# Compact weight and right-hand-side tails in a chain of attention and two gated feed-forward layers

## The chip, the cores and the metric

The kernel runs on one core of a Trainium2 chip. The metric is the device time of one execution in microseconds; the median of several runs counts. TensorE (PE) multiplies matrices, VectorE (DVE) and ScalarE (ACT) work on elements, SyncE (SP) issues nearly all transfers from one queue, in order.

## The reference

```python
x = mlstm(q, k, v, i_gate, f_gate, o_gate)       # (4, 8, 768, 40) -> 3072 tokens x 320
g = sigmoid(x @ moe_w_gate) * (x @ moe_w_val)    # 320 -> 1536
x = g @ moe_w_out                                # 1536 -> 320
h = x @ moe2_w_in                                # 320 -> 2048
y = (h * clip(h + 3, 0, 6) / 6) @ moe2_w_out     # 2048 -> 320
```

`mlstm` is an attention-like recurrence over 768 steps with decays, for 32 heads; it is computed in six chunks of 128 steps.

## The kernel before

Every matmul takes its operands as a high and a low part (`hi` is a cast, `lo` the value minus the cast), and three products of parts are added. An inner size of 320 is two full blocks of 128 rows and a tail of 64; the tail's high and low parts are stacked into one operand of 128 rows.

First come the chunks 0 to 5. In chunk c the steps (c, f), f from 0 to 11, do the first layer: `m1_h` (lines 552 to 559), the gate (line 578, 579), `split_g`, and one or two steps later `m1_out` (lines 594, 604). `m1_end(c)` copies the three output banks into the tile `x2` with line 610 and lines 613 to 615 and stores it in `x2_dram`; it is emitted in step 1 of the next chunk. Between the steps stand pieces of the next chunk's attention (`att0`, `att1`, `att2`: scores, the decays' scan at line 386, their weighing at line 401, transposes at line 534).

Beside this the weights are converted. `work`, one job every second step in the chunks 2 to 4, fetches a pair of 64-bit words, turns it into float32 (`to_f32`, lines 99 to 119) and stores it in `w2_dram` (`store_w2`, line 619): first the eight blocks of `moe2_w_in`, then the eight of `moe2_w_out`. The input layer of the second feed-forward is done in seven products instead of eight for each pair of chunks (a Strassen form of two by two blocks). So each weight block needs four sums (S1 to S4) of its four parts. `combine_w2`, in every second step from chunk 3 on, loads a block back, its tail four times over by transfers of 32 rows (lines 651, 656), forms the sums (line 663), splits them (lines 667, 668, 673) and stores two pieces in `ws_dram` (line 677). The tiles of these pieces, `x2`, and later `w2f` and `o`, have the tag `x2` with two buffers in common.

Then come three pairs of chunks. For each pair seven right-hand sides (`B11`, `B21`, `T1`, `T2`, `B22`, `T3`, `T4`) are formed from `x2_dram`: `x_load` loads four main parts, `x_combine` forms sums (line 843) and splits them (lines 838, 839), and in a second call does the same for the tails, which it loads four times over by transfers of 32 rows (lines 815, 833, 834). For pair 0 this stands in chunk 5, for the others at the end of the pair before. A pair runs eight groups: `load_group` brings the seven weights of a group (line 686), `product` (line 920) multiplies, `gate2` gates, `m2_out` (lines 957 to 959) is the output layer. The gated values of the pair's second chunk are kept and run through `m2_out` at the pair's end, one group after another; there the right-hand sides of the next pair are made.

The order on the engines is a planner's, which takes the program's order as priority and its own estimates of time; `tc.issue_after(gate)` keeps a job behind the gate of its step. A tile with a tag waits for the release of the buffer that it takes.

Of the kernel before, what the change touches and what calls it, by code (L numbers as in the profile page):

```python
# [24 lines left out]
P = 128  # L25
# [7 lines left out]
def mlstm_then_two_gated_ffn(  # L33
# [51 lines left out]
    w2_dram = dram.tile([F2, P, 640], F32, name="w2_dram")  # L85
    ws_dram = dram.tile([F2 // 2, P, 7, 3 * P], F32, name="ws_dram")
# [17 lines left out]
    def to_f32(r, u=None):  # L104

        lower = r.bitcast(I32).rearrange("p (n two) -> p two n", two=2)[:, 0, :]
        u = scaled(r) if u is None else u
        bits = cpool.tile([P, 640], I32, tag="bits", name="bits")
        nc.vector.tensor_scalar(
            out=bits, in0=u.bitcast(I32), scalar1=3, scalar2=None, op0=ALU.logical_shift_left
        )
        nc.vector.scalar_tensor_tensor(
            out=bits, in0=lower, scalar=29, in1=bits,  # L120
            op0=ALU.logical_shift_right, op1=ALU.bitwise_or,
        )
        return bits.bitcast(F32)
# [35 lines left out]
    def hi_out1(key, x):  # L159

        w = new_slot(key)
        nc.scalar.copy(out=w[:, :, 0:320], in_=x.rearrange("p (j n) -> p j n", j=2))
        return w

    def lo_out1(w, x):
        wf = w.bitcast(F32)
        r = x.rearrange("p (j n) -> p j n", j=2)
        nc.vector.tensor_tensor(
            out=w[:, :, 320:384], in0=r[:, :, 256:320], in1=wf[:, :, 256:320], op=ALU.subtract
        )  # L170
        nc.vector.tensor_tensor(
            out=w[:, :, 384:640], in0=r[:, :, 0:256], in1=wf[:, :, 0:256], op=ALU.subtract
        )
# [444 lines left out]
    def store_w2(n, x):  # L618
        nc.sync.dma_start(out=w2_dram[n], in_=x)
# [7 lines left out]
    for n in [*range(0, F2, 2), *range(1, F2, 2)]:  # L627
        jobs.append(((wo2 if n % 2 else w2)[n // 2], store_w2, n))
# [9 lines left out]
    def load_out2(n):  # L638
        x = xpool.tile([P, 640], F32, tag="x2", name="w2f")
        nc.sync.dma_start(out=x, in_=w2_dram[2 * n + 1])  # L640
        split_out2(("out2", n), x)

    A11, A12, A21, A22, S1, S2, S4 = range(7)
    S3 = A21

    def combine_w2(n):


        src = w2_dram[2 * n]
        a = cpool.tile([P, 7, 2, P], F32, tag="wa", name="wa", bufs=1)  # L650
        nc.sync.dma_start(
            out=a[:, 0:4, 0, :], in_=src[:, 0:512].rearrange("p (ik c) -> p ik c", c=P)
        )
        tail = src[:, 512:640].rearrange("(ik r) c -> r ik c", r=32)
        for r in range(0, P, 32):
            nc.sync.dma_start(out=a[r : r + 32, 0:4, 1, :], in_=tail)
        for to, x, y, op in (
            (S1, A21, A22, ALU.add),
            (S2, S1, A11, ALU.subtract),
            (S3, A11, A21, ALU.subtract),  # L660
            (S4, A12, S2, ALU.subtract),
        ):
            nc.vector.tensor_tensor(out=a[:, to], in0=a[:, x], in1=a[:, y], op=op)
        for k, m in ((0, 4), (4, 3)):
            st = xpool.tile([P, 4, 3, P], F32R, tag="x2", name="ws")
            sf = st.bitcast(F32)
            nc.scalar.copy(out=st[:, :m, 0:3:2, :], in_=a[:, k : k + m])
            nc.vector.tensor_tensor(
                out=st[:, :m, 1, :], in0=a[:, k : k + m, 0, :], in1=sf[:, :m, 0, :], op=ALU.subtract
            )  # L670
            for r in (32, 96):
                q = slice(r, r + 32)
                nc.vector.tensor_tensor(
                    out=st[q, :m, 2, :], in0=a[q, k : k + m, 1, :], in1=sf[q, :m, 2, :],
                    op=ALU.subtract,
                )
            nc.sync.dma_start(
                out=ws_dram[n, :, k : k + m, :],
                in_=sf[:, :m].rearrange("p s t c -> p s (t c)"),
            )  # L680
# [3 lines left out]
    def load_group(n):  # L684
        t = xpool.tile([P, 7, 3, P], F32R, tag="x", name="wg")
        nc.sync.dma_start(
            out=t.bitcast(F32).rearrange("p s t c -> p s (t c)"), in_=ws_dram[n]
        )
        w_groups.append(t)
# [101 lines left out]
    combined = 0  # L791

    def x_load(pair):


        def rows():
            return late.tile([P, T], F32, tag="c", name="xr", bufs=11)

        main, tail = {}, {}
        for k in range(2):  # L800
            for j in range(2):
                src = x2_dram[2 * pair + j]
                main[k, j], tail[k, j] = rows(), None
                nc.sync.dma_start(out=main[k, j], in_=src[:, k, :])
        return pair, main

    def x_combine(loads, tail):
        pair, b = loads
        if tail:
            b = {}  # L810
            for k in range(2):
                for j in range(2):
                    b[k, j] = late.tile([P, T], F32, tag="c", name="xr", bufs=11)
                    for r in range(0, P, 32):
                        nc.sync.dma_start(
                            out=b[k, j][r : r + 32],
                            in_=x2_dram[2 * pair + j, 32 * k : 32 * k + 32, 2, :],
                        )
        else:
            xsets.append(  # L820
                {
                    key: late.tile([P, 3, T], F32R, tag="X", name="X", bufs=7)
                    for key in ("B11", "B21", "T1", "T2", "B22", "T3", "T4")
                }
            )
        xs = xsets[-1]
        b11, b12, b21, b22 = b[0, 0], b[0, 1], b[1, 0], b[1, 1]

        def put(key, v):
            x = xs[key]  # L830
            xf = x.bitcast(F32)
            if tail:
                nc.scalar.copy(out=x[:, 2, :], in_=v)
                nc.vector.tensor_tensor(
                    out=x[64:, 2, :], in0=v[64:], in1=xf[64:, 2, :], op=ALU.subtract
                )
            else:
                nc.scalar.copy(out=x[:, 0, :], in_=v)
                nc.vector.tensor_tensor(out=x[:, 1, :], in0=v, in1=xf[:, 0, :], op=ALU.subtract)

        def minus(x, y, out=None):
            out = late.tile([P, T], F32, tag="c", name="xr", bufs=11) if out is None else out
            nc.vector.tensor_tensor(out=out, in0=x, in1=y, op=ALU.subtract)
            return out

        put("B11", b11)
        put("B21", b21)
        t1 = minus(b12, b11)
        put("T1", t1)
        t2 = minus(b22, t1)  # L850
        put("T2", t2)
        put("B22", b22)
        put("T3", minus(b22, b12, b12))
        put("T4", minus(b21, t2))

# [10 lines left out]
    for i, (c, f, ts) in enumerate(steps):  # L866
# [20 lines left out]
        if c == 0:  # L887
            work(1 if i < 2 * halves[0] else 2, n_w1)
        elif c < NC - 1:

            with tc.issue_after(gate):
                work(c > 1 and f % 2 == 0, n_jobs)
                if c > 2 and f % 2 and combined < F2 // 2:
                    combine_w2(combined)
                    combined += 1
        elif f == 0:
            assert not jobs and not pieces and combined == F2 // 2
            early_sb.close()
            late = ctx.enter_context(tc.tile_pool(name="late", bufs=1, reuse_waits="tile"))
            x_loads = x_load(0)  # L900
            load_group(0)
        else:
            if f > 1 and f - 2 < F2 // 2:
                load_out2(f - 2)
            if f in (2, 5):
                x_combine(x_loads, f > 2)
# [10 lines left out]
    def product(ps, w, s, x, first):  # L917

        for i, (a, b) in enumerate(((2, 2), (0, 1), (1, 0), (0, 0))):
            nc.tensor.matmul(  # L920
                out=ps, lhsT=w[:, s, a, :], rhs=x[:, b, :], start=first and i == 0, stop=i == 3,
                skip_group_check=True,
            )

    def sbuf_copy(ps):
        t = late.tile([P, T], F32, tag="c", name="c", bufs=11)
        nc.scalar.copy(out=t, in_=ps)
        return t
# [47 lines left out]
    for pair in range(NC // 2):  # L976
# [4 lines left out]
        for n in range(NG):  # L981
# [30 lines left out]
            if n == NG - 2 and pair + 1 < NC // 2:  # L1012
                x_loads = x_load(pair + 1)
# [6 lines left out]
        for n in range(NG):  # L1020
            for j in range(2):
                m2_out(cb, n, j, split_g(kept[n][:, j]))
            if more and n in (0, 2):
                x_combine(x_loads, n > 0)
# [6 lines left out]
def _layout(q, k, v, i_gate, f_gate, o_gate, moe_w_gate, moe_w_val, moe_w_out, moe2_w_in, moe2_w_out):  # L1031
# [17 lines left out]

    def pairs(w):  # L1050
# [5 lines left out]
    w2 = moe2_w_in.reshape(DM, F2 // 2, 2, P)  # L1056
# [6 lines left out]
        "w2": words(rows_in(w2[:, :, 0].reshape(DM, -1), w2[:, :, 1].reshape(DM, -1))),  # L1063
# [23 lines left out]
```

## Time and profile before

| | |
|---|---|
| median of 3 runs | 861.96 us (860.65 to 863.66) |
| profiled execution, its own time | 860.47 us |
| its span, first to last instruction | 858.6 us |
| PE, DVE, ACT busy share | 97%, 70%, 48% |
| mean granted clock | 0.997 |

The span is what the trace covers. Busy shares are means over stages that differ: chunk 2 runs from about 226 us, chunk 3 from about 306, chunk 4 from about 396, chunk 5 to about 524, the pairs from there on. Matmuls are pipelined, so that a single one is shown longer (0.39 us for 512 columns) than the distance to the next one.

### The profile page before, as it was taken

To read this page: it belongs to the slowest core of one execution; us is meant where nothing else is said; L and a number is where in the kernel's file an instruction comes from. 1 tells how busy PE (TensorE), PEld (TensorE's weight loads), DVE (VectorE), ACT (ScalarE), POOL (GpSimd) and SP (SyncE) were. 2 spreads that over 40 slices of the span, in tenths; PEclk is the share of its full clock that TensorE was granted. 3 is DMA by queue.
4 is the path that set the end of the run, shared out by engine and by line. 5 is a ranking of instruction groups with operands and counts; after the bars stand their busy time and mean duration, and the time that the engine had idled before them with its cause. 6 is when DMAs were issued, how large, how long until landed. Compare 5 with 4: busy or idle time off the path is not lost.

```text
span 858.6 us, 17204 instructions
## 1 busy us (share of the span) xinstructions
PE 829.1 (97%) x7109; PEld 710.1 (83%) x7109; DVE 603.7 (70%) x1086; ACT 413.2 (48%) x821; POOL 2.5 (0%) x8
## 2 busy tenths in 40 slices
PE   6599899999999999998999999999999999999998
PEld 6489689888788787786888888888998889988898
DVE  7899975775576678988956734656766668665653
ACT  3687733322333343444425524656546555555542
POOL 1000000000000000000000000000000000000000
PEclk9999999999999999999999999999999999999999
DMA  9635733322555368887623503434404454033300
GB/s 345 234 126 198 260 98 111 126 94 73 173 171 165 124 241 265 274 268 254 208 99 116 156 1 110 177 138 177 144 32 142 159 199 144 32 129 134 124 31 32
DMA packets 41534, 130.65 MB, mean 152 GB/s; under 512 B 4592, under 2 KB 16048, under 8 KB 38384
## 3 DMA queue, kind: packets, MB, share of 16 engines
q1 hardware_dynamic: 41408, 129.45, 43.9%
q8 instruction: 56, 0.92, 0.4%
q14 instruction: 22, 0.18, 0.1%
q10 hardware_dynamic: 48, 0.10, 0.0%
HBM read 104.53 MB, written 25.00 MB: 151 GB/s over the span
## 4 chain that ended last, share of the span: by engine, by line
PE 79%; DVE 13%; DMA 4%; issue 2%; ACT 1%; SPq 0%; DVEq 0%; ACTq 0%
PE acc L594 9%; PE mm L920 9%; PE mm L558 6%; PE mm L556 6%; PE mm L557 6%; PE att L920 4%; PE acc L920 4%; PE mm L552 4%; PE acc L604 3%; PE mm L559 3%; PE mm L959 2%; PE mm L957 2%; PE acc L957 2%; PE mm L958 2%; PE acc L959 2%
## 5 line engine op out<-in xcount | busy, mean ns | idle before, releaser
L565 ACT CAST gh<-g 128x512 fp32r<-128x512 f32 (+1 forms) x130 | 76.4, 588 | 132.2 <-DVE g L579 110.4
L556 PE MATMUL mm<-x,w 128*128 128x512 f32 (+1 forms) x328 | 121.0, 369 | 0.0
L557 PE MATMUL mm<-x,w 128*128 128x512 f32 (+1 forms) x328 | 120.8, 368 | 0.0
L558 PE MATMUL mm<-x,w 128*128 128x512 f32 (+1 forms) x328 | 120.4, 367 | 0.0
L566 DVE TENSOR_TENSOR gl<-g,gh 128x512 fp32r<-128x512 f32 (+1 forms) x130 | 84.1, 647 | 51.2 <-ACT gh L565 50.8
L594 PE MATMUL acc<-gh,w 128*128 128x512 f32 (+1 forms) x328 | 104.4, 364 | 0.1
L920 PE MATMUL mm<-X,wg 128*128 128x512 f32 x336 | 84.3, 391 | 0.0
L579 DVE TENSOR_TENSOR g<-g,mm 128x512 f32<-128x512 f32 (+1 forms) x82 | 50.4, 615 | 34.6 <-PE mm L559 34.2
L920 PEld LDWEIGHTS mm<-X,wg 128*128 128x128 f32 x336 | 61.9, 188 | 12.6 <-DVE g L936 0.3
L557 PEld LDWEIGHTS mm<-x,w 128*128 128x128 f32 x328 | 62.8, 191 | 10.7
L558 PEld LDWEIGHTS mm<-x,w 128*128 128x128 f32 x328 | 62.6, 191 | 10.6
L556 PEld LDWEIGHTS mm<-x,w 128*128 128x128 f32 x328 | 62.8, 191 | 8.4
L594 PEld LDWEIGHTS acc<-gh,w 128*128 128x128 f32 x328 | 60.6, 189 | 10.7 <-ACT x L610 0.9
L552 PE MATMUL mm<-x,w 128*128 128x512 f32 (+1 forms) x164 | 66.8, 408 | 2.5 <-DVE cst L523 1.6
L578 ACT ACTIVATE g<-mm 128x512 f32<-128x512 f32 (+1 forms) x82 | 44.5, 543 | 44.0 <-PE mm L559 41.8
L386 DVE TENSOR_TENSOR_SCAN dec<-dec,ident 128x512 f32<-128x512 f32 x40 | 48.0, 1215 | 21.3 <-DMA dec<-fz_dram 21.3
L559 PE MATMUL mm<-x,w 128*128 128x512 f32 (+1 forms) x164 | 59.9, 365 | 0.0
L594 PE MATMUL acc<-gl,w 128*128 128x512 f32 (+1 forms) x164 | 59.8, 365 | 0.0
L935 ACT ACTIVATE gb<-c,half 128x512 f32<-128x512 f32 x48 | 34.6, 724 | 44.0 <-DVE c L931 43.7
L566 DVE TENSOR_TENSOR gl<-gb,gh 128x512 fp32r<-128x512 f32 x48 | 32.4, 690 | 24.2 <-ACT gh L565 24.1
L565 ACT CAST gh<-gb 128x512 fp32r<-128x512 f32 x48 | 29.5, 620 | 36.5 <-PE att L958 35.1
L920 PE MATMUL att<-X,wg 128*128 128x512 f32 x168 | 46.3, 395 | 0.0
(188 smaller groups left out, 1737.9 us busy)
## 6 DMA issues: line engine op xcount, KB each, us to landing
wg<-ws_dram SPq DMA_DIRECT2D x24, 1344.0 KB, 5.7
raw<-in_w SPq DMA_DIRECT2D x20, 640.0 KB, 4.3
qk<-in_qkT SPq DMA_DIRECT2D x22, 512.0 KB, 5.0
vko<-in_vko SPq DMA_DIRECT2D x22, 480.0 KB, 4.4
dec<-fz_dram SPq DMA_DIRECT2D x20, 512.0 KB, 5.8
raw<-in_wo SPq DMA_DIRECT2D x14, 640.0 KB, 4.5
ws_dram<-ws SPq DMA_DIRECT2D x8, 768.0 KB, 3.6
w_dram<-bits SPq DMA_DIRECT2D x16, 320.0 KB, 2.4
```

Source lines behind the costliest of these rows:

```text
L386: nc.vector.tensor_tensor_scan(out=x, data0=a["factors"][n] if "factors" in a else x, data1=ident4.rearrange("p h l -> p (h l)"), initial= ...
L552: nc.tensor.matmul(out=banks[j], lhsT=tail, rhs=xl[:, 2, :], start=True, stop=False)
L556: nc.tensor.matmul(out=banks[j], lhsT=hi, rhs=xh[:, k, :], start=False, stop=False)
L557: nc.tensor.matmul(out=banks[j], lhsT=hi, rhs=xl[:, k, :], start=False, stop=False)
L558: nc.tensor.matmul(out=banks[j], lhsT=lo, rhs=xh[:, k, :], start=False, stop=False)
L559: nc.tensor.matmul(out=banks[j], lhsT=tail, rhs=xh[:, 2, :], start=False, stop=True)
L565: nc.scalar.copy(out=gh, in_=g)
L566: nc.vector.tensor_tensor(out=gl, in0=g, in1=gh.bitcast(F32), op=ALU.subtract)
L578: gate = nc.scalar.activation(out=g, in_=banks[0], func=AF.Sigmoid).ins
L579: nc.vector.tensor_tensor(out=g, in0=g, in1=banks[1], op=ALU.mult)
L594: nc.tensor.matmul(out=a[m], lhsT=lhsT, rhs=rhs, start=st and lhsT is hi and rhs is gh, stop=en and lhsT is lo, skip_group_check=True,)
L920: nc.tensor.matmul(out=ps, lhsT=w[:, s, a, :], rhs=x[:, b, :], start=first and i == 0, stop=i == 3, skip_group_check=True,)
```

## The change

The layout of `moe2_w_in` on the host puts the tail of each block as 4 x 32 rows of 32 columns beside its four main parts, so that the four parts lie in one tile [128, 7 x 160] after conversion, with room for the three sums. `combine_w2` is now the job's own second half: it takes the converted tile, with no way through DRAM, and forms four sums of 160 columns. It writes all high parts to one tile and all low parts to another, and stores of each the main part in `ws_dram` and the tail in rows 0 to 31 or 32 to 63 of `wt_dram`. `load_group` reads the main parts with one transfer and the stack of 64 rows twice.

The jobs alternate between a block of `moe2_w_in` and one of `moe2_w_out`; the extra calls in the chunks 3 and 4 are gone. For the right-hand sides `x_load` loads the tails packed as [128, 128] beside the main parts, sums are formed over 640 columns, and `put` splits the packed tail, stores it in `xt_dram` and reads it back with four transfers into the 128 rows of its operand. `x_combine` is a generator that makes one right-hand side at each call, one per step of chunk 5 and one per group at a pair's end. The tag `c` has 7 buffers of 640 columns instead of 11 of 512.

```diff
+    wt_dram = dram.tile([F2 // 2, 64, 7, P], F32, name="wt_dram")
+    xt_dram = dram.tile([NC // 2, 7, 2, 4, 32, P], F32, name="xt_dram")
+    ws_dram = dram.tile([F2 // 2, P, 2, 7 * P], F32, name="ws_dram")
...
-        bits = cpool.tile([P, 640], I32, tag="bits", name="bits")
+        tile_ = cpool.tile([P, 7 * 160], I32, tag="bits", name="bits")
+        bits = tile_[:, 0:640]
...
+    def combine_w2(n, x):
+        a = x.rearrange("p (s c) -> p s c", s=7)
         for to, x, y, op in (
             (S1, A21, A22, ALU.add),
             (S2, S1, A11, ALU.subtract),
...
             (S4, A12, S2, ALU.subtract),
         ):
             nc.vector.tensor_tensor(out=a[:, to], in0=a[:, x], in1=a[:, y], op=op)
+        hi, lo = [xpool.tile([P, 7 * 160], F32R, tag="x2", name="ws") for _ in range(2)]
+        main, tail = [
+            (a[:, :, k:m], [t[:, 7 * k : 7 * m].rearrange("p (s c) -> p s c", s=7) for t in (hi, lo)])
+            for k, m in ((0, P), (P, 160))
+        ]
+        for v, (h, _) in (main, tail):
+            nc.scalar.copy(out=h, in_=v)
+        for v, (h, l) in (main, tail):
+            nc.vector.tensor_tensor(out=l, in0=v, in1=h.bitcast(F32), op=ALU.subtract)
+        for k, t in enumerate((hi, lo)):
+            tf = t.bitcast(F32)
+            nc.sync.dma_start(out=ws_dram[n, :, k], in_=tf[:, : 7 * P])
+            nc.sync.dma_start(
+                out=wt_dram[n, 32 * k : 32 * k + 32].rearrange("r s (q c) -> q r s c", q=4),
+                in_=tf[:, 7 * P :].rearrange("p (s c) -> p s c", s=7),
             )
...
+    for n in range(F2 // 2):
+        jobs.append((w2[n], combine_w2, n))
+        jobs.append((wo2[n], store_w2, n))
...
+        t = xpool.tile([P, 3, 7, P], F32R, tag="x", name="wg")
+        tf = t.bitcast(F32).rearrange("p a s c -> p a (s c)")
+        nc.sync.dma_start(out=tf[:, 0:2], in_=ws_dram[n])
+        for r in (0, 64):
             nc.sync.dma_start(
+                out=tf[r : r + 64, 2], in_=wt_dram[n].rearrange("r s c -> r (s c)")
             )
...
+                t = b[k, j] = late.tile([P, 640], F32, tag="c", name="xr", bufs=7)
+                nc.sync.dma_start(out=t[:, 0:T], in_=src[:, k, :])
+                for q in range(4):
+                    nc.sync.dma_start(
+                        out=t[32 * q : 32 * q + 32, T:],
+                        in_=src[32 * k : 32 * k + 32, 2, q * P : (q + 1) * P],
+                    )
+        return x_combine(pair, b)
...
+        def put(key, v):
+            x = xs[key] = late.tile([P, 3, T], F32R, tag="X", name="X", bufs=7)
+            t = late.tile([P, 2, P], F32R, tag="xt", name="xt", bufs=3)
+            xf, tf = x.bitcast(F32), t.bitcast(F32)
+            nc.scalar.copy(out=t[:, 0, :], in_=v[:, T:])
+            nc.vector.tensor_tensor(out=t[:, 1, :], in0=v[:, T:], in1=tf[:, 0, :], op=ALU.subtract)
+            d = xt_dram[pair, len(xs) - 1]
+            nc.sync.dma_start(out=d.rearrange("k q r t -> (q r) k t"), in_=tf)
+            for k in range(4):
+                nc.sync.dma_start(
+                    out=xf[32 * k : 32 * k + 32, 2, :].rearrange("r (q t) -> r q t", q=4),
+                    in_=d[k // 2].rearrange("q r t -> r q t"),
+                )
+            nc.scalar.copy(out=x[:, 0, :], in_=v[:, 0:T])
+            nc.vector.tensor_tensor(
+                out=x[:, 1, :], in0=v[:, 0:T], in1=xf[:, 0, :], op=ALU.subtract
             )
...
-                if c > 2 and f % 2 and combined < F2 // 2:
-                    combine_w2(combined)
-                    combined += 1
...
-            if f in (2, 5):
-                x_combine(x_loads, f > 2)
+            next(x_parts, None)
...
-            if more and n in (0, 2):
-                x_combine(x_loads, n > 0)
+            if more:
+                next(x_parts, None)
```

## Rows read from the trace of the kernel before

**Rows 1.** The page, busy time of the engines over the span.

```profile
PE 829.1 (97%) x7109; PEld 710.1 (83%) x7109; DVE 603.7 (70%) x1086; ACT 413.2 (48%) x821; POOL 2.5 (0%) x8
```

**Rows 2.** Busy time by stretch: length, PE, PEld, DVE, ACT, POOL, granted clock, DMA share, GB/s.

```profile
226.00:306.00 80.00, 80.00 (x878) 64.01 (x877) 55.52 (x105) 28.30 (x58) 0.00 (x0) 1.00 0.50 164
306.00:330.00 24.00, 24.00 (x248) 19.12 (x248) 19.63 (x37) 12.63 (x23) 0.00 (x0) 1.00 0.69 236
330.00:372.00 42.00, 40.93 (x432) 32.73 (x432) 39.74 (x76) 17.38 (x34) 0.00 (x0) 1.00 0.79 262
372.00:402.00 30.00, 27.62 (x225) 20.86 (x223) 28.45 (x51) 12.98 (x23) 0.00 (x0) 0.94 0.80 272
```

**Rows 3.** Waits of TensorE from 300 to 402 us: total, times, longest.

```profile
PE att L534 <- DVE dec L401: 3.2, 2, 2.2
```

**Rows 4.** TensorE in order of time: start, length, instruction, idle time before it.

```profile
396.04 0.55 PE L534 MATMUL att<-ident,yo 128*128 128x128 f32 x3 [2.23 <-DVE dec L401]
...
398.42 0.63 PE L557 MATMUL mm<-x,w 128*128 128x512 f32 x1
399.19 0.80 PE L594 MATMUL acc<-gh,w 128*128 128x512 f32 x1
```

**Rows 5.** Busy time by stretch, behind the stall (columns as in rows 2).

```profile
396.00:400.00 4.00, 3.83 (x11) 2.62 (x12) 4.00 (x6) 2.36 (x6) 0.00 (x0) 0.57 0.82 284
```

**Rows 6.** The chain that ended last, around 395 us: start, length, what.

```profile
393.00 5.53 DMA ws_dram<-ws
...
398.55 0.59 ACT x L610
```

**Rows 7.** Busy time by stretch, end of the first pair (columns as in rows 2).

```profile
600.00:636.00 36.00, 35.18 (x233) 34.23 (x232) 26.93 (x44) 19.26 (x35) 0.00 (x0) 1.00 0.27 87
```

**Rows 8.** Busy time on tiles `wa` (twice) and `xr`: DVE, ACT, clock, DMA share, GB/s.

```profile
200.00:460.00 260.00, 41.85 (x80) 14.38 (x16) 0.99 0.58 195
...
306.00:402.00 96.00, 29.88 (x56) 10.81 (x12) 0.98 0.77 259
...
430.00:745.00 315.00, 43.62 (x66) 24.81 (x42) 1.00 0.35 122
```

**Rows 9.** Groups of VectorE by shape: busy us, mean ns, idle before.

```profile
L179 DVE TENSOR_TENSOR w<-w2f,w 128x640 fp32r<-128x640 f32 x8 | 6.6, 823 | 5.1 <-ACT w L178 5.1
...
L168 DVE TENSOR_TENSOR w<-bits,w 128x128 fp32r<-128x128 f32 x6 | 1.7, 278 | 0.0
```

**Rows 10.** Waits from 160 to 163 us.

```profile
PE att L534 <- DVE dec L401: 1.6, 1, 1.6
```

**Rows 11.** Transfers by line: count, KB each, median us from issue to landing.

```profile
w_dram<-bits SPq DMA_DIRECT2D x16, 320.0 KB, 2.4
...
xr<-x_dram SPq DMA_DIRECT2D x48, 64.0 KB, 2.1
...
wa<-w_dram SPq DMA_DIRECT2D x8, 256.0 KB, 5.5
wa<-w_dram SPq DMA_DIRECT2D x32, 64.0 KB, 4.2
```

**Rows 12.** ScalarE in order of time, change from chunk 2 to chunk 3.

```profile
296.70 0.60 ACT L578 ACTIVATE g<-mm 128x512 f32<-128x512 f32 x1 [2.25 <-PE mm L559]
...
306.48 0.59 ACT L610 COPY x<-acc 128x512 f32<-128x512 f32 x1 [1.58 <-PE acc L594]
...
308.69 0.58 ACT L614 COPY sw<-acc 64x512 f32<-64x512 f32 x1
```

**Rows 13.** TensorE in order of time, first output product of chunk 3.

```profile
312.40 0.39 PE L594 MATMUL acc<-gh,w 128*128 128x512 f32 x1
```

**Rows 14.** Line 815, issues on SP's queue: ns min/median/max.

```profile
L815 SPq DMA_DIRECT2D xr<-x_dram x48: 302/419/1837, 456.7 to 726.3; - x48
```

**Rows 15.** SP's queue in order of time, last groups of the first pair.

```profile
583.97 1.95 SPq L804 DMA_DIRECT2D xr<-x_dram  x4
593.81 10.23 SPq L686 DMA_DIRECT2D wg<-ws_dram  x2
```

More of the change, by code (lines that the diff above doesn't have):

```diff
@@ L84, in mlstm_then_two_gated_ffn @@
     x2_dram = dram.tile([NC, P, 3, T], F32, name="x2_dram")
-    w2_dram = dram.tile([F2, P, 640], F32, name="w2_dram")
-    ws_dram = dram.tile([F2 // 2, P, 7, 3 * P], F32, name="ws_dram")
+    wo2_dram = dram.tile([F2 // 2, P, 640], F32, name="wo2_dram")
+    wt_dram = dram.tile([F2 // 2, 64, 7, P], F32, name="wt_dram")
+    xt_dram = dram.tile([NC // 2, 7, 2, 4, 32, P], F32, name="xt_dram")
+    ws_dram = dram.tile([F2 // 2, P, 2, 7 * P], F32, name="ws_dram")
     slots = {}
@@ L122, in to_f32 @@
         )
-        return bits.bitcast(F32)
+        return tile_.bitcast(F32)
     def new_slot(key):
@@ L161, in hi_out1 @@
         w = new_slot(key)
-        nc.scalar.copy(out=w[:, :, 0:320], in_=x.rearrange("p (j n) -> p j n", j=2))
+        nc.scalar.copy(out=w[:, :, 0:320], in_=x[:, 0:640].rearrange("p (j n) -> p j n", j=2))
         return w
@@ L166, in lo_out1 @@
         wf = w.bitcast(F32)
-        r = x.rearrange("p (j n) -> p j n", j=2)
+        r = x[:, 0:640].rearrange("p (j n) -> p j n", j=2)
         nc.vector.tensor_tensor(
@@ L618, in store_w2 @@
     def store_w2(n, x):
-        nc.sync.dma_start(out=w2_dram[n], in_=x)
+        nc.sync.dma_start(out=wo2_dram[n], in_=x[:, 0:640])
+    A11, A12, A21, A22, S1, S2, S4 = range(7)
+    S3 = A21
+    def combine_w2(n, x):
+        a = x.rearrange("p (s c) -> p s c", s=7)
+        for to, x, y, op in (
+            (S1, A21, A22, ALU.add),
+            (S2, S1, A11, ALU.subtract),
+            (S3, A11, A21, ALU.subtract),
+            (S4, A12, S2, ALU.subtract),
+        ):
+            nc.vector.tensor_tensor(out=a[:, to], in0=a[:, x], in1=a[:, y], op=op)
+        hi, lo = [xpool.tile([P, 7 * 160], F32R, tag="x2", name="ws") for _ in range(2)]
[14 more added lines that the diff above has]
+            )
     jobs = []
@@ L626, in mlstm_then_two_gated_ffn @@
     n_w1 = len(jobs)
-    for n in [*range(0, F2, 2), *range(1, F2, 2)]:
-        jobs.append(((wo2 if n % 2 else w2)[n // 2], store_w2, n))
+    for n in range(F2 // 2):
+        jobs.append((w2[n], combine_w2, n))
+        jobs.append((wo2[n], store_w2, n))
     jobs.reverse()
@@ L639, in load_out2 @@
         x = xpool.tile([P, 640], F32, tag="x2", name="w2f")
-        nc.sync.dma_start(out=x, in_=w2_dram[2 * n + 1])
+        nc.sync.dma_start(out=x, in_=wo2_dram[n])
         split_out2(("out2", n), x)
[L643 to L680, printed above, removed]
     w_groups = []
     def load_group(n):
[L685 to L688, printed above, removed]
+        t = xpool.tile([P, 3, 7, P], F32R, tag="x", name="wg")
[5 more added lines that the diff above has]
+            )
         w_groups.append(t)
@@ L790, in mlstm_then_two_gated_ffn @@
     xsets = []
-    combined = 0
     def x_load(pair):
-        def rows():
-            return late.tile([P, T], F32, tag="c", name="xr", bufs=11)
-        main, tail = {}, {}
+        b = {}
         for k in range(2):
@@ L802, in x_load @@
                 src = x2_dram[2 * pair + j]
[L803 to L824, printed above, removed]
-            )
[L826 to L839, printed above, removed]
@@ new lines, in x_load, with x_combine @@
+                t = b[k, j] = late.tile([P, 640], F32, tag="c", name="xr", bufs=7)
[4 more added lines that the diff above has]
+                        in_=src[32 * k : 32 * k + 32, 2, q * P : (q + 1) * P],
+                    )
+        return x_combine(pair, b)
+    def x_combine(pair, b):
+        b11, b12, b21, b22 = b[0, 0], b[0, 1], b[1, 0], b[1, 1]
+        xs = {}
+        xsets.append(xs)
+        def put(key, v):
[7 more added lines that the diff above has]
+            for k in range(4):
+                nc.sync.dma_start(
+                    out=xf[32 * k : 32 * k + 32, 2, :].rearrange("r (q t) -> r q t", q=4),
+                    in_=d[k // 2].rearrange("q r t -> r q t"),
+                )
+            nc.scalar.copy(out=x[:, 0, :], in_=v[:, 0:T])
+            nc.vector.tensor_tensor(
+                out=x[:, 1, :], in0=v[:, 0:T], in1=xf[:, 0, :], op=ALU.subtract
+            )
@@ L841, in minus @@
         def minus(x, y, out=None):
-            out = late.tile([P, T], F32, tag="c", name="xr", bufs=11) if out is None else out
+            out = late.tile([P, 640], F32, tag="c", name="xr", bufs=7) if out is None else out
             nc.vector.tensor_tensor(out=out, in0=x, in1=y, op=ALU.subtract)
@@ L846, in x_combine @@
         put("B11", b11)
+        yield
         put("B21", b21)
+        yield
         t1 = minus(b12, b11)
         put("T1", t1)
+        yield
         t2 = minus(b22, t1)
         put("T2", t2)
+        yield
         put("B22", b22)
+        yield
         put("T3", minus(b22, b12, b12))
-        put("T4", minus(b21, t2))
+        yield
+        put("T4", minus(b21, t2, b21))
+        yield
     n_two = n_first + len(tile_steps(1))
@@ L892, in mlstm_then_two_gated_ffn @@
                 work(c > 1 and f % 2 == 0, n_jobs)
-                if c > 2 and f % 2 and combined < F2 // 2:
-                    combine_w2(combined)
-                    combined += 1
         elif f == 0:
-            assert not jobs and not pieces and combined == F2 // 2
+            assert not jobs and not pieces
             early_sb.close()
             late = ctx.enter_context(tc.tile_pool(name="late", bufs=1, reuse_waits="tile"))
-            x_loads = x_load(0)
+            x_parts = x_load(0)
             load_group(0)
@@ L920, in product @@
             nc.tensor.matmul(
-                out=ps, lhsT=w[:, s, a, :], rhs=x[:, b, :], start=first and i == 0, stop=i == 3,
+                out=ps, lhsT=w[:, a, s, :], rhs=x[:, b, :], start=first and i == 0, stop=i == 3,
                 skip_group_check=True,
@@ L925, in sbuf_copy @@
     def sbuf_copy(ps):
-        t = late.tile([P, T], F32, tag="c", name="c", bufs=11)
+        t = late.tile([P, 640], F32, tag="c", name="c", bufs=7)[:, 0:T]
         nc.scalar.copy(out=t, in_=ps)
@@ L1012, in mlstm_then_two_gated_ffn @@
             if n == NG - 2 and pair + 1 < NC // 2:
-                x_loads = x_load(pair + 1)
+                x_parts = x_load(pair + 1)
         more = pair + 1 < NC // 2
@@ L1048, in rows_in, with rows_combined @@
         return np.concatenate([main, tail], axis=2)
+    def rows_combined(w):
+        w = w.reshape(DM, -1, 2, P)
+        main = w[: 2 * P].reshape(2, P, -1, 2, P).transpose(2, 1, 3, 0, 4)
+        tail = w[2 * P :].reshape(2, 32, -1, 2, 4, 32).transpose(2, 4, 1, 3, 0, 5)
+        n = main.shape[0]
+        parts = [main.reshape(n, P, 4, P), tail.reshape(n, P, 4, 32)]
+        return np.concatenate(parts, axis=3).reshape(n, P, 640)
     def pairs(w):
@@ L1054, in words @@
         return np.ascontiguousarray(w).view(np.int64)
-    w2 = moe2_w_in.reshape(DM, F2 // 2, 2, P)
     return {
@@ L1062, in _layout @@
         "wo1": words(pairs(moe_w_out)),
-        "w2": words(rows_in(w2[:, :, 0].reshape(DM, -1), w2[:, :, 1].reshape(DM, -1))),
+        "w2": words(rows_combined(moe2_w_in)),
         "wo2": words(pairs(moe2_w_out)),
```

## The prediction

> **What bounds the kernel now.** The engine table of the page comes first: TensorE is busy 829.1 of 858.6 us [rows 1]. The change touches no matmul: the same products, with the same shapes, read the same values from another place. It can therefore only give back time in which TensorE waits, or add some. The second view is the busy time by stage [rows 2]. From 226 to 330 us TensorE has no idle time at all; from 330 to 402 it loses 1.07 and 2.38 us. In the two stretches that lose, VectorE (DVE) is busy 39.74 of 42 and 28.45 of 30 us, 95% of both; in the two that don't, it is at 69 and 82%. That is the reading on which this prediction rests: over the whole span VectorE is no bound, but it is the bound for these 72 us, and that is where the combinations of the weights stand (line 663 and lines 667 to 673).
>
> The third view says what those waits were. TensorE waited twice for line 401, the weighing of the scores on VectorE, 3.2 us in all [rows 3]; the longer wait is 2.23 us, ahead of the transposes at 396.04 [rows 4]. Behind the stall the clock falls: from 396 to 400 us the granted clock is 0.57 of full, a mixture of the two levels of 1.2 and 2.4 GHz, so 4.0 x 0.43 = 1.7 us more are lost [rows 5]. The chain of waits shows a second cause at the same place: the store of a combined weight, issued at 393.00, takes 5.53 us, and ScalarE's copy at line 610 starts only when it has landed [rows 6], because the copied tile has the store's tile as its buffer; line 594 on TensorE starts behind that copy, at 399.19, 0.77 us after the matmul before it [rows 4]; I put 0.3 us of that down to the copy, the rest to the slow clock. The sum that this stage loses: 3.2 + 1.7 + 0.3 = 5.2 us. More than that the change can hardly win. What else TensorE waits for lies in the first 161 us, where it adds nothing, or at the end of the pairs (36.00 - 35.18 = 0.8 us each [rows 7]), where a gate's own chain ends.
>
> **The weights' half.** Eight combinations cost VectorE 41.85 us and ScalarE 14.38 [rows 8], so 5.23 and 1.80 each. An operation's price over its columns comes from two rows with 128 and 640 columns, 0.278 and 0.823 us [rows 9]: 0.142 us + 1.064 ns a column. After: four sums of 160 columns at 0.312 = 1.25 us, one subtraction of 896 at 1.095, one of 224 at 0.38: 2.73 us, 2.5 less per combination. ScalarE casts 1120 columns instead of 1792: 1.1 instead of 1.8 us. Where they stand matters more. Before, six fall into one chunk (306 to 402 us); after, each stands behind its conversion in the same job, three in chunk 2, three in chunk 3, two in chunk 4. In the 96 us from 306 to 402, VectorE's 19.63 + 39.74 + 28.45 = 87.8 us hold 29.88 us of the combinations' work [rows 2, 8]; with four in their place (the first of chunk 4 starts within them) it is 87.8 - 29.9 + 10.9 = 68.8, or 72%. Chunk 2 (226 to 306 us) goes from 55.5 to 55.5 + 8.2 = 63.7 of 80, 80%. Both lie below the 82% at which TensorE didn't wait. So VectorE's backlog goes, and the lateness of line 401 with it.
>
> Not all of that wait need go. At 160 us TensorE waits 1.6 us for the same line 401 where no combination stands [rows 10]. On SP's queue a job now has four stores in place of one store, five loads and two stores; they wait for ScalarE and VectorE as those did, with the attention's loads queued behind them, for whose decays line 401 waits in turn. Four issues fewer and 40 loads of 4 MB less [rows 11] speak for earlier loads, not later ones. I keep 0.5 us of the 5.2 as left over.
>
> **The tails' stores.** Two of the four stores go in runs of 32 values: 4 x 32 x 7 = 896 runs of 128 bytes. The trace has no such run. The nearest rows: 64 KB in 32 runs land in 2.1 us, 64 KB in 128 runs in 4.2, 256 KB in 512 runs in 5.5 [rows 11]. From the first to the second a run costs (4.2 - 2.1) / 96 = 22 ns, from the second to the third 1.3 / 384 = 3.4 ns; that gives 2.1 + 896 x 0.022 = 21.8 us at most and 2.1 + 896 x 0.0034 = 5.1 us at least. I take 5.1, by the row whose number of runs is nearest to 896. What waits for it: `hi`, `lo` and the next chunk's `x2` share two buffers, and the combination of each chunk's step 0 stands one step ahead of line 610's copies into `x2`. On ScalarE the next step's sigmoid is queued behind those copies, and TensorE waits for both. Chunk 3 gives the times: its step 0 converts behind the gate at 296.70 [rows 12]; I estimate 6 us for conversion, combination, casts and the issue of both stores of `hi`, so 302.9. Line 610 starts at 306.48, the last copy of that block ends at 308.69 + 0.58 = 309.27 [rows 12], and TensorE takes the bank again at 312.40 [rows 13]. So the copies may start 3.1 us late, at 309.6: a store that lands within 309.6 - 302.9 = 6.7 us costs nothing. With 5.1 us it is covered, by 1.6 us. If that cover goes, each of three chunk changes pays the excess.
>
> **The right-hand sides' half.** VectorE spent 43.62 us and ScalarE 24.81 on them [rows 8]. After: 12 differences of 640 columns (0.823), 21 subtractions of 512 (0.687) and 21 of 128 (0.278): 9.9 + 14.4 + 5.8 = 30.1 us, 13.5 less. At a pair's end VectorE is busy 26.93 of 36 us while TensorE loses 0.8 [rows 7], so this is worth nothing. SP's queue pays for it: each tail is now stored and read back by four transfers. Seven tails a pair are 7 x 5 issues of 0.42 us [rows 14] and seven waits for a store, 2.4 us each as the store of converted weights [rows 11]: 7 x (2.1 + 2.4) = 31.5 us. While SP waits, the next tail, a group's load or an output's store is queued behind it. The stage has 36 us, and the work can start before it: the sixteen tail loads now go with the four main loads, 20 x 0.42 = 8.4 us from 583.97 in a queue that had nothing else to issue until 593.81 [rows 15]. The seventh tail is read by the seventh product of the next pair, not at its start; pair 0 has chunk 5, twice as long. Cost 0, with the last tail's way as the other bound: 2.4 + 4 x 0.42 + 2.1 = 6.2 us a pair. Seven buffers of 640 columns in place of eleven hold four loads and one group's three copies, just enough, and `load_group` issues three transfers a whole group ahead: 0 both.
>
> **The sum.** 5.2 - 0.5 = 4.7 us less, from 860.47 to 855.8 us for the profiled execution, whose own time is 1.49 us under the median of the runs. Against the median: 861.96 - 4.7 = 857.3 us. A measurement of this kernel tells about 0.3%, 2.6 us, from no change.
>
> **Rivals.** First, the wait comes back elsewhere: line 401 is late because its decays are, as at 160 us [rows 10], or the copies of line 610 wait at more chunk changes than before. Against it: VectorE had hardly a pause in the stretches that lost. Some 2 us of gain stay: 860 us.
>
> Second, slower: the tails' stores land late. If the 896 runs of a store pass through a quarter of the DMA engines, the 3.0 us that they take above the first 2.1 become 12, and a store lands in 14.1 us. Line 610 is then 14.1 - 6.7 = 7.4 us too late at three chunk changes: 22.2 - 4.7 = 17.5 us slower, 879 us. It outweighs the gain from a landing of 6.7 + 4.7 / 3 = 8.3 us. For it: line 610 waits for such a store already [rows 6], and the upper bound is 21.8 us. Against: the planner may put the copies ahead of the combination, and 22 ns a run comes from loads that went beside others. The Trainium skill speaks for it ("DMA: Bandwidth & Descriptors", the section on why a DMA increments its semaphore by 16 and not by 1): a transfer runs on the largest number of engines up to 16 that divides the slowest dimension of both sides, here 4 on the DRAM side, so on 4 of 16. By that rule the time is this rival's 879 us; no run here shows a transfer whose slowest dimension is under 16.
>
> Third, the right-hand sides' round trip is too long, and the last tails come late at two pair starts. At half the bound, 3 us each, it is 857.3 + 6 = 863.3 us.
>
> **Chances and range.** Forecast (4.7 us, give or take 2) 0.53; first rival 0.21; third 0.08; second 0.18. Faster by over 0.3% is the forecast, 0.53; within 0.3% the first and third, 0.29; slower the second, 0.18. The range runs from the whole 5.2 us and the median's scatter of 1.3 us below it, 855.4, to a landing of 9.6 us, 3 x (9.6 - 8.3) = 4 us above the time before, 866. Alone, the forecast's own range is 855.4 to 859.3.
>
> **What would show it.** Right: TensorE without idle time and at full clock from 306 to 402 us, VectorE near 72% there and near 80% in chunk 2, no wait of line 610 for a store. Wrong: line 610 waiting for `ws_dram` or `wt_dram` near 230, 306 or 395 us; tails' stores that land over 8 us; idle time ahead of line 920's products at the start of pair 1 or 2. The prediction fails outright if the planner, given other operations, orders the attention's pieces later.

## The result and the profile after

The changed kernel takes 871.99 us (median of 5 runs, 868.24 to 873.55); the kernel before took 863.66 in runs on the same chip (861.96 in the three shown above). The ratio is 1.0108, 95% interval 1.0088 to 1.0128: slower by 1.1%. The prediction was 857.3 us, 855.4 to 866, and 0.53 for faster. The profiled execution took 873.55 us, the most of the five, and its span is 871.8 against 858.6. So the two traces lie 13.2 us apart where the medians of the runs lie 8.3 apart; what follows explains the two traces.

The page's table of engines, after:

```profile
PE 834.2 (96%) x7109; PEld 714.4 (82%) x7109; DVE 568.9 (65%) x1042; ACT 400.8 (46%) x821; POOL 2.5 (0%) x8
```

VectorE lost 34.8 us of work and ScalarE 12.4 [rows 1], as the change meant, and still the kernel became slower. Busy time by stretch, after (columns as in [rows 2]):

```profile
226.00:306.00 80.00, 75.42 (x724) 59.76 (x723) 53.33 (x101) 27.67 (x56) 0.00 (x0) 0.96 0.53 173
306.00:330.00 24.00, 22.80 (x260) 17.69 (x258) 16.50 (x33) 9.33 (x19) 0.00 (x0) 1.00 0.55 178
330.00:372.00 42.00, 41.77 (x537) 33.50 (x538) 31.53 (x61) 15.71 (x33) 0.00 (x0) 1.00 0.57 189
372.00:402.00 30.00, 26.18 (x204) 20.95 (x203) 18.35 (x39) 8.52 (x18) 0.00 (x0) 0.89 0.50 159
```

From 306 to 402 us VectorE is at 69%, near the predicted 72% and far from the 95% in two of the three stretches before. Yet TensorE idles 4.6 us in chunk 2, where it had no pause, and 3.8 us from 372 to 402. The waits of TensorE from 220 to 430 us, after (total, times, longest):

```profile
PE att L363 <- DVE x L543: 7.1, 2, 3.8
PE att L456 <- DVE x L543: 3.3, 2, 2.1
PE att L537 <- DVE dec L404: 0.9, 2, 0.7
PE acc L607 <- DVE x L618: 0.6, 1, 0.6
```

That is 11.9 us of waits where there were 3.2 [rows 3]. Behind three of them, of 3.3, 3.8 and 2.1 us, the clock falls. The granted clock is the third number from the end:

```profile
297.20:304.00 6.80, 5.31 (x22) 4.41 (x23) 4.82 (x8) 0.98 (x2) 0.00 (x0) 0.50 0.47 147
386.00:392.60 6.60, 5.41 (x22) 4.51 (x23) 4.03 (x7) 0.69 (x2) 0.00 (x0) 0.50 0.40 134
420.00:423.40 3.40, 3.40 (x9) 2.62 (x9) 2.84 (x8) 0.36 (x2) 0.00 (x0) 0.50 0.78 264
```

Three stretches at the lower level, 1.2 GHz, 16.8 us together, cost 8.4 us if TensorE works all through them, where one cost 1.7 [rows 5]. But TensorE still idles in the first two, up to 1.5 and 1.2 us by the busy column, so waits and clock overlap: 11.9 + 8.4 less some 1.3 (half of that idle time) is 19.0 us, and the 5.2 us of before go off: 13.8 estimated against 13.2 measured. All of it lies in the chunks. From chunk 1's store of `x2` to chunk 5's there were 533.24 - 233.79 = 299.5 us before and are 547.37 - 234.40 = 313.0 now.

Line 543 is VectorE's last step of an attention piece, line 404 the weighing that was line 401. What VectorE itself waits for is plain from the chain of waits (start, length, what):

```profile
289.25 4.60 DMA dec<-fz_dram
293.85 0.02 issue
293.87 1.23 DVE dec L389
295.10 0.58 DVE g L582
...
298.19 0.46 DVE x L543
298.65 0.04 issue
298.69 2.07 PE att L363 x14
```

Between 288.7 and 293.87 us VectorE does nothing: its next instruction is the scan over decays whose load was issued only at 289.25. It has work behind that scan (line 582, whose inputs are there) but takes its queue in order. SP's queue in order of time shows why the load came so late:

```profile
280.91 0.33 SPq L650 DMA_DIRECT2D ws_dram<-ws  x1
281.33 0.53 SPq L651 DMA_DIRECT2D wt_dram<-ws  x1
282.04 3.20 SPq L650 DMA_DIRECT2D ws_dram<-ws  x1
285.33 0.54 SPq L651 DMA_DIRECT2D wt_dram<-ws  x1
285.97 3.18 SPq L212 DMA_DIRECT2D qk<-in_qkT  x1
289.25 0.38 SPq L223 DMA_DIRECT2D dec<-fz_dram  x1
```

The issue of a tail's store (line 651) takes 0.5 us, but what is issued right behind it takes 3.2 us here and 2.9 to 4.5 at the other combinations, whether it is a store or a load; the same lines take 0.33 us otherwise. Two tails a combination hold SP up for some 6 us, and the attention's loads stand right behind. The load of the decays is itself no slower than before: its median from issue to landing is 5.0 us, against 5.9. Over 220 to 430 us VectorE's scan waits 24.4 us for decays, where it waited 9.6 (after, then before, where line 386 is the same scan):

```profile
DVE dec L389 <- DMA dec<-fz_dram: 24.4, 8, 5.8
...
DVE dec L386 <- DMA dec<-fz_dram: 9.6, 5, 4.6
```

While only a tail is being stored, the DMA share (before the last number) is a quarter:

```profile
345.50:347.50 2.00, 2.00 (x11) 1.64 (x10) 1.31 (x3) 0.98 (x3) 0.00 (x0) 1.00 0.26 41
```

The share is a mean over 16 engines, and 0.26 x 16 = 4.2, so I estimate that about four of them work. That agrees with the rule that the second rival cited from the Trainium skill, "DMA: Bandwidth & Descriptors", the section on why a DMA increments its semaphore by 16 and not by 1.

### The profile page after: what moved, and what is told of

It is laid out like the page before. It is cut to its first block, busy times and chain, and to the rows that moved or that the text cites. A ratio compares the mean times of both kernels' runs of the same rounds, so it can differ in the third digit from the quotient of the medians.

```text
span 871.8 us, 17379 instructions
## 1 busy us (share of the span) xinstructions
PE 834.2 (96%) x7109; PEld 714.4 (82%) x7109; DVE 568.9 (65%) x1042; ACT 400.8 (46%) x821; POOL 2.5 (0%) x8
## 4 chain that ended last, share of the span: by engine, by line
PE 82%; DVE 8%; DMA 7%; issue 2%; ACT 1%; SPq 0%; DVEq 0%; ACTq 0%
PE mm L913 9%; PE acc L597 9%; PE mm L559 6%; PE mm L561 6%; PE mm L560 6%; DMA dec<-fz_dram 5%; PE att L913 5%; PE acc L913 4%; PE mm L555 4%; PE mm L562 3%; PE acc L607 3%; PE att L363 3%; DVE dec L389 2%; PE mm L950 2%; PE mm L951 2%; PE acc L950 2%
## 5 line engine op out<-in xcount | busy, mean ns | idle before, releaser
L928 ACT ACTIVATE gb<-c,half 128x512 f32<-128x512 f32 x48 | 34.8, 725 | 45.6 <-DVE c L924 45.3
```

## The experiments

Theory A: the stores of the tails hold up SP's queue and the attention's loads behind it. Theory B: what hurts is line 613 (610 before), waiting for a buffer until the tail has landed; it waited 10.3 us in three. Theory C: the combinations' new place disturbs the attention's work on VectorE, whatever the stores do. Each ratio below is to the kernel before, run on the same chip. Unless it is said otherwise, the edits are to the changed kernel.

### The tails' store, three ways

Contiguous, at the price of scrambled tails:

```diff
-                out=wt_dram[n, 32 * k : 32 * k + 32].rearrange("r s (q c) -> q r s c", q=4),
-                in_=tf[:, 7 * P :].rearrange("p (s c) -> p s c", s=7),
+                out=wt_dram[n, 32 * k : 32 * k + 32]
+                .rearrange("r s c -> (r s c)")
+                .rearrange("(p x) -> p x", p=P),
+                in_=tf[:, 7 * P :],
```

> The changed kernel, but each tail goes to wt_dram as it lies in the tile, 128 runs of 896 bytes instead of 896 runs of 128 bytes; same bytes, same number of stores, same order of issues. The weights' tails are then scrambled, only the time counts. Theory A (the stores in short runs hold up SP's queue, the attention's decays come late, TensorE waits): the issue behind a tail's store takes 0.33 us instead of some 3, the waits for dec go back to a few us, and the time is 857 to 860 us. Theory B (line 613 waits for the shared buffer until the tail has landed): also about 858 to 862, since the store lands sooner. Theory C (the new place of the combinations disturbs the attention's work on VectorE, whatever the stores do): 868 to 873, as the changed kernel.

852.62 us, ratio 0.9899 (0.9882 to 0.9915). Theory C falls: with the combinations in the same place the kernel is 1% faster than before. This store has fewer runs and another slowest dimension at once, so it doesn't tell the two apart. The four quarters each by itself:

```diff
-            nc.sync.dma_start(
-                out=wt_dram[n, 32 * k : 32 * k + 32].rearrange("r s (q c) -> q r s c", q=4),
-                in_=tf[:, 7 * P :].rearrange("p (s c) -> p s c", s=7),
-            )
+            for q in range(4):
+                nc.sync.dma_start(
+                    out=wt_dram[n, 32 * k : 32 * k + 32, :, 32 * q : 32 * q + 32],
+                    in_=tf[32 * q : 32 * q + 32, 7 * P :].rearrange("p (s c) -> p s c", s=7),
+                )
```

> The changed kernel, but each tail's store is four transfers of 32 rows x 7 x 32 values: the same 896 runs of 128 bytes in all, with a slowest dimension of 32 instead of 4. If the number of runs sets the hold-up on SP's queue (about 3 ns a run): again some 3 us per tail plus six issues more per combination, 870 to 875 us. If it is that a store with slowest dimension 4 uses few DMA engines: four issues of about 0.45 us, no hold-up behind them, landing in 3 to 4 us, 858 to 863 us.

854.95 us, ratio 0.9917 (0.9902 to 0.9932), with six issues more for each combination. The same short runs go to the same places in DRAM, so neither their sum nor where they go is the cause; that each transfer is smaller stays open. The cleanest test alters the layout alone: rows outermost among the 128 partitions, sums outermost in `wt_dram`. Then row and quarter merge into one dimension of 128, and the store is one transfer again. I call this the mended kernel. The order on TensorE, VectorE and ScalarE is that of the changed kernel, instruction for instruction but for two neighbouring matmuls.

```diff
-    wt_dram = dram.tile([F2 // 2, 64, 7, P], F32, name="wt_dram")
+    wt_dram = dram.tile([F2 // 2, 7, 64, P], F32, name="wt_dram")
...
-                out=wt_dram[n, 32 * k : 32 * k + 32].rearrange("r s (q c) -> q r s c", q=4),
+                out=wt_dram[n, :, 32 * k : 32 * k + 32].rearrange("s r (q c) -> (r q) s c", q=4),
...
-                out=tf[r : r + 64, 2], in_=wt_dram[n].rearrange("r s c -> r (s c)")
+                out=t.bitcast(F32)[r : r + 64, 2], in_=wt_dram[n].rearrange("s r c -> r s c")
...
-        tail = w[2 * P :].reshape(2, 32, -1, 2, 4, 32).transpose(2, 4, 1, 3, 0, 5)
+        tail = w[2 * P :].reshape(2, 32, -1, 2, 4, 32).transpose(2, 1, 4, 3, 0, 5)
```

> The changed kernel with one thing altered: the tails lie as (row, quarter) instead of (quarter, row) on the 128 partitions and wt_dram has the sum outermost, so that the store is again one transfer of 896 runs of 128 bytes, but with a slowest dimension of 128 instead of 4; order and shapes of all work on TensorE, VectorE and ScalarE are the same, the group's tail loads now read 448 runs of 512 bytes each. If the slowest dimension of 4 is the cause (few DMA engines, whose rings fill up and hold SP's queue): issue of the transfer behind it 0.3 to 0.6 us, landing 2 to 4 us, no wait of line 613, 851 to 855 us. If the number of runs in one transfer is the cause, and splitting helped because each part was small: hold-up of some 3 us and landing of 6 us as before, 868 to 873 us.

853.67 us, ratio 0.9906 (0.9885 to 0.9928). SP's queue at the same place, the stages, and the DMA share while only a tail is being stored:

```profile
277.91 0.33 SPq L650 DMA_DIRECT2D ws_dram<-ws  x1
278.32 0.39 SPq L651 DMA_DIRECT2D wt_dram<-ws  x1
279.04 0.56 SPq L650 DMA_DIRECT2D ws_dram<-ws  x1
279.69 0.44 SPq L651 DMA_DIRECT2D wt_dram<-ws  x1
280.61 1.03 SPq L212 DMA_DIRECT2D qk<-in_qkT  x1
281.73 0.51 SPq L223 DMA_DIRECT2D dec<-fz_dram  x1
```

```profile
226.00:306.00 80.00, 80.00 (x878) 64.32 (x878) 61.12 (x119) 31.53 (x64) 0.00 (x0) 1.00 0.58 190
306.00:402.00 96.00, 96.00 (x1019) 77.04 (x1018) 69.82 (x132) 37.44 (x75) 0.00 (x0) 1.00 0.59 190
...
336.50:337.00 0.50, 0.50 (x4) 0.39 (x3) 0.50 (x2) 0.50 (x2) 0.00 (x0) 1.00 0.91 134
```

From the first store to the decays' issue it is 3.8 us instead of 8.3, with the same 896 runs of 128 bytes. TensorE has no idle time from 226 to 402 us and its full clock; VectorE is at 76 and 73%, and its scan waits 11.2 us for decays. Tails land in 3.7 us (median). The store differs from the changed kernel's in its slowest dimension, 128 instead of 4, and so in its DMA share, 0.91 instead of 0.26. The read-back differs too, but it begins at 450 us, behind all of this.

### Fewer engines still, and long runs on four

```diff
-            nc.sync.dma_start(
-                out=wt_dram[n, 32 * k : 32 * k + 32].rearrange("r s (q c) -> q r s c", q=4),
-                in_=tf[:, 7 * P :].rearrange("p (s c) -> p s c", s=7),
-            )
+            for q in (0, 2):
+                nc.sync.dma_start(
+                    out=wt_dram[n, 32 * k : 32 * k + 32, :, 32 * q : 32 * q + 64].rearrange("r s (q c) -> q r s c", q=2),
+                    in_=tf[32 * q : 32 * q + 64, 7 * P :].rearrange("p (s c) -> p s c", s=7),
+                )
```

> The changed kernel with each tail's store cut into two transfers of two quarters: 448 runs of 128 bytes each, slowest dimension 2. If the slowest dimension sets the number of engines: each transfer has 224 runs on each of two engines, as many as the changed kernel has on four, so each holds up SP for some 3 us, four a combination in place of two, 12 us instead of 6: 880 to 900 us, DMA share an eighth while they run. If only the number of runs in a transfer counts: half the hold-up for each, the same sum, about 872 us.

899.8 us, ratio 1.0421 (1.0393 to 1.0449), the top of what was expected. At the same place it is 12.6 us from the first store to the decays' issue, so 8.8 more than in the mended kernel, where the changed kernel has 4.5 more. The loss against the mended kernel is 2.5 times that of the changed one, 5.2 and 2.0% of the time before. From 220 to 470 us the scan waits 34.0 us for decays, TensorE 9.6 for line 404 and 9.4 for line 543. While only tails are being stored, the DMA share is 0.20:

```profile
299.10:303.40 4.30, 4.30 (x22) 3.49 (x21) 2.00 (x4) 0.63 (x1) 0.00 (x0) 1.00 0.20 23
```

That is lower than 0.26, as expected, but not the eighth that two engines would give. So the share orders the three stores (0.91, 0.26, 0.20) and doesn't count the engines exactly. Long runs with a slowest dimension of 4:

```diff
-    wt_dram = dram.tile([F2 // 2, 64, 7, P], F32, name="wt_dram")
+    wt_dram = dram.tile([F2 // 2, 2, 4, 33, 7 * 32], F32, name="wt_dram")
...
-            nc.sync.dma_start(
-                out=wt_dram[n, 32 * k : 32 * k + 32].rearrange("r s (q c) -> q r s c", q=4),
-                in_=tf[:, 7 * P :].rearrange("p (s c) -> p s c", s=7),
-            )
+            nc.sync.dma_start(out=wt_dram[n, k, :, 0:32], in_=tf[:, 7 * P :])
...
-        for r in (0, 64):
+        for r in (0, 32, 64, 96):
```

> The changed kernel with tails' stores of 128 runs of 896 bytes and a slowest dimension of 4 (a padded layout keeps the four quarters apart); the tails are read back in four transfers and lie in another order of columns, so only the time counts. If few DMA engines alone do the harm: DMA share of about a quarter while a tail is stored and SP held up, 860 us or more. If it takes few engines and many short runs, that is many descriptors on each engine (32 here instead of 224): no hold-up, 852 to 856 us.

869.0 us, ratio 1.008 (1.0058 to 1.0103), which would speak for few engines as the whole cause; the trace says otherwise. The stores do use few engines (DMA share 0.30 from 336.5 to 337.0 us), yet from 220 to 530 us TensorE waits once, for 0.5 us, and chunk 1's store of `x2` to chunk 5's takes 527.29 - 232.54 = 294.8 us, as in the mended kernel (526.42 - 230.60 = 295.8). The loss stands in the pairs, which now read four pieces a group. Waits of TensorE from 520 us on:

```profile
PE acc L948 <- ACT gh L568: 5.0, 4, 2.1
PE mm L948 <- ACT gh L568: 4.1, 2, 2.1
```

In the mended kernel these are 1.2 and 0.8 us. The planner also gave the pairs another order here: of the 7109 matmuls 386 behind 527 us stand in another place than in the mended kernel. So 128 long runs with a slowest dimension of 4 are harmless in the chunks where 896 short ones are not: it takes few engines and many runs. Whether the loss in the pairs comes from the read-back or from the other order stays open.

### Theory B

```diff
-            nc.sync.dma_start(
+            nc.gpsimd.dma_start(
                 out=wt_dram[n, 32 * k : 32 * k + 32].rearrange("r s (q c) -> q r s c", q=4),
```

> The changed kernel, but the tails' stores are issued by the idle GpSimd, the same runs and the same layout. Theory A: SP's queue is free of the hold-up, decays land in time, 857 to 861 us, even if the stores themselves land later than before (7 us or more) and line 613 waits for them. Theory B: the stores land no sooner, so line 613 waits as long or longer, 870 us or more. Theory C: 868 to 873.

866.97 us, ratio 1.0066 (1.0042 to 1.009), between what the theories A and B gave. SP is free (the issues of line 650 take 0.33 us), but a tail lands only after 9.5 us (median), and now TensorE waits for line 613. Waits from 220 to 430 us:

```profile
ACT x L613 <- DMA wt_dram<-ws: 19.9, 3, 7.3
DVE dec L389 <- DMA dec<-fz_dram: 16.2, 8, 3.5
...
PE acc L597 <- ACT x L613: 4.6, 2, 2.9
```

Here is the path that the second rival described, with its three chunk changes. Why the scan still waits 16.2 us this run doesn't show. In the changed kernel itself line 613 waits too, but it isn't what costs:

```diff
-        hi, lo = [xpool.tile([P, 7 * 160], F32R, tag="x2", name="ws") for _ in range(2)]
+        hi = cpool.tile([P, 7 * 160], F32R, tag="hi", name="ws", bufs=1)
+        lo = xpool.tile([P, 7 * 160], F32R, tag="x2", name="ws")
```

> The changed kernel, but the high parts' tile has a buffer of its own, so that line 613's copies share two buffers with the low parts alone. SP's queue is as before. Theory A: the waits of line 613 for wt_dram (10.3 us in three) go or shrink, the two stalls at about 295 and 383 us (3.3 and 3.9 us, both with a slow clock behind) stay, 866 to 870 us. Theory B: most of the loss goes, 858 to 862 us. Theory C: 868 to 873.

872.63 us, ratio 1.0134 (1.0113 to 1.0154), no better than the changed kernel. Line 613 waits for no tail any more, and the scan still waits for decays (in the changed kernel, then in this one):

```profile
ACT x L613 <- DMA wt_dram<-ws: 10.3, 3, 4.2
...
DVE dec L389 <- DMA dec<-fz_dram: 23.7, 8, 5.5
```

My own figure of 866 to 870 was too low as well: TensorE's waits from 220 to 430 us are 12.0 us in all, as many as the 11.9 of the changed kernel.

### The halves, and the place of the combinations

The right-hand sides' half put into the kernel before (its lines of the diff and nothing else):

```diff
...
-            if f in (2, 5):
-                x_combine(x_loads, f > 2)
+            next(x_parts, None)
...
```

> The kernel before with the right-hand sides' half of the change alone (packed tails, stored and read back, 7 buffers). If that half is free, as predicted, or only takes work out of the gate's chain at the pairs' ends: 0 to 1 us less than before, 859.5 to 863. If the round trip costs: idle time ahead of line 920's products at the start of the second and third pair, 1 to 6 us more than before.

861.24 us, ratio 0.9995 (0.9982 to 1.0007): free, as predicted. The weights' half with the mended store, right-hand sides as in the kernel before:

```diff
...
-            next(x_parts, None)
+            if f in (2, 5):
+                x_combine(x_loads, f > 2)
...
```

> The weights' half alone, with the store whose slowest dimension is 128, and the right-hand sides as before. If the gain of the mended kernel comes from the weights' half: 852 to 857 us. If the right-hand sides' half carries part of it (fewer operations ahead of the last gate of a pair): 1 us more than the kernel with both halves.

854.75 us, ratio 0.9918 (0.9896 to 0.994): all of the gain, within what the runs tell apart. The mended kernel with the jobs in their old order:

```diff
     for n in range(F2 // 2):
         jobs.append((w2[n], combine_w2, n))
+    for n in range(F2 // 2):
         jobs.append((wo2[n], store_w2, n))
```

> The mended kernel (slowest dimension 128), but with the eight conversions and combinations of the input weights one after another, six in chunk 2 and two in chunk 3, and those of the output weights behind them, as the jobs stood before. If VectorE's backlog is what a dense row of combinations costs: VectorE some 72 of 80 us busy in chunk 2, TensorE waits 2 to 5 us there, 854 to 859 us. If compact combinations are cheap enough anywhere: within 1 us of the mended kernel.

858.45 us, ratio 0.9965 (0.9946 to 0.9984), so 0.6 of the 0.9% gained are gone. The time lies within what was expected, the reason doesn't: VectorE is at 63.74 of 80 us in chunk 2, not at some 72. TensorE waits 2.0 us from 220 to 430 us. The profiled execution took 856.53 us, 1.9 less than the median, so its trace shows only part of the loss, and what the order costs stays open. And the last, a buffer of its own for the high parts in the mended kernel:

```diff
+        hi = cpool.tile([P, 7 * 160], F32R, tag="hi", name="ws", bufs=1)
+        lo = xpool.tile([P, 7 * 160], F32R, tag="x2", name="ws")
```

> The mended kernel (slowest dimension 128) with a buffer of its own for the high parts' tile. If the shared buffers still cost anything (line 613 waited 2.6 us for a tail once): up to 1 us less, 852 to 854 us. If that wait is covered, as TensorE's trace without idle time says: the same as the mended kernel.

853.68 us, ratio 0.9898 (0.9881 to 0.9916): nothing left there. The best kernels are this one and the mended kernel, 1% under the kernel before.

## Why the prediction was wrong

**What held.** VectorE as the bound of 330 to 402 us, and the waits there as what the change can win: with the store mended TensorE has no pause from 226 to 402 us. VectorE's share was worked out as 72% there and 80% in chunk 2; the mended kernel shows 73% and 76%. The right-hand sides' half costs nothing. The size came out too small: the gain was taken as 4.7 us, and the mended kernel's ratio is worth 8.1 us of 862.2. Its profiled span is 7.2 us shorter. Matmul by matmul beside the trace of before (the n-th beside the n-th), it is 0.5 us ahead at 330 us, 2.2 at 350 and 6.8 behind 402. So the stage gave back 6.3 us, where the prediction had added up 5.2, and nothing of the 0.5 us kept back was left over.

**What failed** is the part on the tails' stores, twice. It priced a store by the number of its runs and took 5.1 us from the row with 512 runs; the trace has one that landed after 6.64 us, and from GpSimd's queue the median is 9.5. The rows were of transfers whose slowest dimension is 32 or 128. What they could not show, how a transfer is spread over the DMA engines, decided. And it let the store cost only by its landing, at line 610. The wait there came, as its signs of being wrong said (10.3 us in three), but it is not what cost: without it the kernel is no faster. The prediction named the attention's loads as queued behind the stores on SP, then counted issues and found four fewer. That an issue can be held up by the transfer ahead of it stood at nothing, without a reason, and it is the main price: some 6 us on SP for each combination, decays that are issued 4.5 us later than in the mended kernel (at the place shown), and 11.9 us of waits on TensorE. What in the queue holds the issue no trace shows. A hint was in the trace before: the loads of line 656 behind a load of 512 runs took up to 1.68 us to issue instead of 0.46.

**The second rival** had the cause, a quarter of the engines, and a chance of 0.18. Its path was the lesser one and its 879 us were too much: at 6.6 us the landing itself is still below the 6.7 us that I took as harmless, and at the chunk changes TensorE waited only 0.6 us (for line 618, which follows line 613's copies). The rule of the Trainium skill that it cited was right about the spread in this case (DMA share 0.26); I gave the row that was nearest in one property (runs) more weight than a rule on another property (spread) that no row could contradict.

## What to carry to other kernels

Read the slowest dimension of every transfer's two sides before its bytes: 4 there meant about four DMA engines of 16, and a layout that merges it into 128 turned 1.1% of loss into 0.9% of gain. Price a transfer on an in-order queue by what it does to the issue behind it as well as by its landing, and look at what that next issue is for. Work taken off an engine that is the bound of one stage was worth that stage's waits and the slow clock behind them, and a late load handed them back at once.

## What was not expected of the hardware

Right behind a store of 896 runs with a slowest dimension of 4, the next issue on SP's queue takes 2.9 to 4.5 us in the changed kernel. With a slowest dimension of 128 and the same runs it takes 0.5 to 2.0 us in the mended kernel; with 128 runs and a slowest dimension of 4, 0.3 to 2.1 us. The changed kernel's store issued by GpSimd lands after 9.5 us (median of 16) instead of 6.6 (one store). The two longest waits of TensorE in the changed kernel, 3.3 and 3.8 us, are followed by 6.8 and 6.6 us at 1.2 GHz. Matmul by matmul beside the trace of before, they cost 6.2 and 6.4 us, nearly twice their length; a wait of 2.1 us is followed by 3.4 us at 1.2 GHz.
